# A listed order of steps, replaced by another list, in a one-core kernel of linear attention and a cos-gated MLP

## The chip, the core and the metric

The kernel runs on one core of a Trainium2 chip. The core has TensorE (PE, matmuls and transposes), VectorE (DVE), ScalarE (ACT), GpSimd (POOL) and SyncE (SP), each with its own queue of instructions, which it works off in order. DMAs are issued by SP, ACT and POOL. The metric is the device time of one execution in microseconds; smaller is better.

## What is computed

All inputs are float32. First linear attention for 8 batches, 8 heads, 576 rows and 64 columns, then an MLP on the 4608 rows of 512 that come of it:

```python
def _attn_ref(q, k, v):
    q_s = np.exp(q - np.max(q, axis=-1, keepdims=True))
    q_s = q_s / (np.sum(q_s, axis=-1, keepdims=True) + 1e-09)
    k_s = np.exp(k - np.max(k, axis=2, keepdims=True))
    k_s = k_s / (np.sum(k_s, axis=2, keepdims=True) + 1e-09)
    kv = np.einsum('bhsd,bhse->bhde', k_s, v)
    return np.einsum('bhsd,bhde->bhse', q_s, kv)

def _moe_ref(x, w_in, w_out):
    h = x @ w_in
    g = h * np.cos(h)
    return g @ w_out
```

Between the two, heads and columns are joined to rows of 512. w_in is 512 x 2048, w_out 2048 x 512.

## The kernel before

x is worked off in nine blocks of 512 rows: blocks 0 to 7 are the first 512 rows of each batch, block 8 the 64 rows left of all eight. The attention of a batch runs in two halves of four heads (a = 0, 1; the tiles are `q_0`, `q_1`, `k_0`, `k_1`), and the MLP of a block runs over chunks of 128 of the 2048 hidden columns: h (L1058 at the start, L1066 later), the gate on ACT and DVE (L1091, L1095, L1101, L1106), and its product with w_out into four banks `acc` (L1144, L1151). But for the start, float32 products are made of parts in fp32r: a high and a low part of each operand (`ghi` L1122, `glo` L1126), three matmuls for one. Blocks 5 to 8 are done as two pairs, by seven products of half-size sums in place of eight (L1438 `z` and `a`, with weights and sums of them that are put into DRAM as `w_own` and `w_sums` and loaded back as `s`).

The steps of a half of a batch's attention: `q_max` (L804), then for batch 0's first half 18 exponentials on ACT, each with its own bias and sum (`q_exps`, L817), for all others `q_sub` (L808), one exponential (L812) and a sum (L823); `q_inv` (L827, L828) and `q_norm` (L832). For k: its maximum over rows by three steps on DVE (L694, L699, L703), POOL's all-reduce over partitions (L709, two to a half), `k_sub` (L716) and the exponential (L722). `kv` (L760) multiplies v and k; v has columns of ones beside it, from which `kv_inv` (L768 to L770) makes the divisor, and ACT scales kv by it into `kvw` (L774). q is transposed by PE in batches 0 and 1 (L861, copied by ACT in L865), later by DVE in squares of 32 (`q_blocks`, L880 and L885), through DRAM (`q_rows`, `q_left`). x is the product of `qf` and `kvw` (L913).

Loads of k, q and v have fixed places in SBUF. 576 rows are 4 chunks of 128 and one of 64, the "left" one; in a tile of k the unused 64 rows of that chunk are filled with the lowest float (`frame` in `load_k`, L612, by DVE for batch 0 and by POOL for the others), and v's ones and zeros are set by `v_frame` (L425 to L428). Each load is a main DMA and a left one (k: L617, L620; q: L635, L639, twice; v: L654, L658). The weights come as `raw_i` (L524) and `raw_o` (L529) and are split by L553, L558, L564 and L575. Before PE has real work it runs matmuls on zeros (L739, L1616).

What sets the order: every step is recorded by `plan.add` or `plan.load` with its engine, a duration, what it reads and writes. `Plan.order` could sort them by a list scheduler, with `Plan.lat` as the latency between two steps. A table `ORDER` of all step numbers stands in the file, and it is used instead:

```python
    steps = ORDER or plan.order(CFG["kappa"], CFG["rounds"], CFG["tables"], CFG["alpha"])
```

The steps are then issued in this order, each to its engine's queue, so the table sets the order on every engine. DMA instructions stand in the queue of the engine that issues them, and an SP that waits for a buffer holds every DMA behind it.

Of the kernel before, what the change touches and what calls it, by code (L numbers as in the profile page):

```python
# [215 lines left out]
class Plan:  # L216
# [48 lines left out]
    def lat(self, i, j):  # L265

        a, b = self.steps[i], self.steps[j]
        return self.LAT.get((a[0], b[0]), (a[7] or 1.1) if a[0] == "BUS" else 0.2)
# [89 lines left out]
def linear_attention_then_cos_gated_mlp(  # L358
# [85 lines left out]
    plan = Plan()  # L444
# [161 lines left out]
    def load_k(b, a, place, due, eng="SP"):  # L606
        places = place if isinstance(place, list) else [(place, i) for i in (0, 1)]
# [1093 lines left out]
```

## Time and profile before

| | us |
|---|---|
| median of 3 runs | 863.61 (862.93 to 864.96) |
| profiled execution, its own time | 862.21 |
| its span in the profile | 860.4 |
| PE busy | 844.9 (98%) |
| DVE busy | 600.3 (70%) |
| ACT busy | 491.9 (57%) |
| POOL busy | 71.4 (8%) |

The span runs from the first to the last record; about 1.8 us of the execution lie around it. Engines wait for each other by semaphores; a row of the waits says which engine sat idle before an instruction, and what ended the idle time. A timeline row gives start and length, and in brackets the idle time before it.

### The profile page before, as it was taken

What the parts mean: (1) busy time and instruction counts of PE and PEld (TensorE: products, weight loads), DVE (VectorE), ACT (ScalarE), POOL (GpSimd) and SP (SyncE); (2) the same over time, 40 slices, a digit from 0 to 9 for tenths busy, and PEclk for the clock granted to TensorE, in tenths of its full rate; (3) what the DMA queues carried; (4) which work ended last, traced back from release to release, by engine and by line L of the source; (5) the groups of instructions that cost most, each with busy time, mean ns of one, the idle gap of its engine ahead of it and who ended that gap; (6) DMA issues with size and microseconds to landing.
All of it is one profiled execution on the core that took longest, in us unless ns stands there. A gap on an engine that the chain in (4) does not pass through costs nothing.

```text
span 860.4 us, 12174 instructions
## 1 busy us (share of the span) xinstructions
PE 844.9 (98%) x4340; PEld 664.6 (77%) x4340; DVE 600.3 (70%) x941; ACT 491.9 (57%) x819; POOL 71.4 (8%) x117
## 2 busy tenths in 40 slices
PE   6999999999999999999999999999999999999997
PEld 5644788877877887877877887887888888888886
DVE  5899889986867775776888886784457655444452
ACT  4788788755545546545654657574446544454441
POOL 1200110000001000001000012111100111101000
PEclk8999999999999999999999999999999999999999
DMA  9882474535554454463578837756333546333204
GB/s 237 260 240 102 145 219 127 157 87 162 136 140 112 109 137 135 117 186 114 136 245 258 271 112 216 201 160 189 98 120 123 159 151 180 86 110 109 63 22 126
DMA packets 152381, 130.32 MB, mean 151 GB/s; under 512 B 65536, under 2 KB 125696, under 8 KB 152320
## 3 DMA queue, kind: packets, MB, share of 16 engines
q1 hardware_dynamic: 135456, 98.47, 40.4%
q0 software_dynamic: 13312, 29.36, 11.6%
q10 hardware_dynamic: 3552, 1.70, 0.8%
q8 instruction: 34, 0.56, 0.3%
q14 instruction: 27, 0.22, 0.1%
HBM read 89.92 MB, written 39.58 MB: 151 GB/s over the span
## 4 chain that ended last, share of the span: by engine, by line
PE 92%; DMA 3%; SPq 1%; ACT 1%; DVE 1%; issue 0%; ACTq 0%; DVEq 0%
PE acc L1151 42%; PE h L1066 21%; PE z L1438 10%; PE a L1438 7%; PE h L1058 3%; PE acc L1144 2%; PE kv L760 2%; PE x L913 2%; DMA q<-in_q_dram 2%; ACT q L817 1%; DVE qm L804 0%; PE acc L739 0%; PE qt L861 0%; PE xl L913 0%; SPq L635 0%
## 5 line engine op out<-in xcount | busy, mean ns | idle before, releaser
L1066 PE MATMUL h<-x,w_i 128*128 128x512 f32 x864 | 207.7, 391 | 1.4 <-DVE kt L1106 1.4
L1066 PEld LDWEIGHTS h<-x,w_i 128*128 128x128 f32 x864 | 161.4, 188 | 36.7 <-DVE kt L1106 2.2
L1151 PE MATMUL acc<-w_o,ghi 128*128 128x512 f32 x592 | 184.7, 393 | 0.0
L1151 PEld LDWEIGHTS acc<-w_o,ghi 128*128 128x128 f32 x592 | 109.7, 188 | 29.8 <-issue 5.7
L1151 PE MATMUL acc<-w_o,glo 128*128 128x512 f32 x296 | 115.4, 390 | 0.0
L1438 PE MATMUL z<-xs,s 128*128 128x512 f32 x384 | 97.6, 390 | 0.2 <-DVE glo L1126 0.2
L1091 ACT ACTIVATE kt<-h 128x512 int32<-128x512 f32 x80 | 47.6, 595 | 81.7 <-PE h L1066 67.6
L1438 PEld LDWEIGHTS z<-xs,s 128*128 128x128 f32 x384 | 71.9, 188 | 15.6 <-DVE glo L1126 0.6
L1438 PE MATMUL a<-xs,s 128*128 128x512 f32 x288 | 73.2, 390 | 0.0
L1095 DVE SCALAR_TENSOR_TENSOR kt<-kt,h 128x512 f32<-128x512 int32 x80 | 54.4, 680 | 27.0 <-ACT kt L1091 26.8
L1101 ACT ACTIVATE kt<-kt 128x512 f32<-128x512 f32 x80 | 50.4, 632 | 32.8 <-DVE kt L1095 31.9
L1151 PEld LDWEIGHTS acc<-w_o,glo 128*128 128x128 f32 x296 | 55.6, 188 | 12.0
L1122 ACT CAST ghi<-kt 128x512 fp32r<-128x512 f32 x74 | 45.1, 616 | 31.9 <-PE acc L1151 25.8
L1438 PEld LDWEIGHTS a<-xs,s 128*128 128x128 f32 x288 | 54.0, 188 | 11.2
L1106 DVE TENSOR_TENSOR kt<-kt,h 128x512 f32<-128x512 f32 x74 | 49.9, 678 | 12.5 <-ACT kt L1101 12.0
L1126 DVE TENSOR_TENSOR glo<-kt,ghi 128x512 fp32r<-128x512 f32 x74 | 50.4, 684 | 8.9 <-ACT ghi L1122 8.9
L709 POOL PARTITION_ALL_REDUCE m<-m x32 | 26.0, 856 | 206.5 <-DVE m L703 193.8
L1452 ACT COPY c<-z 128x512 f32<-128x512 f32 x32 | 18.7, 586 | 39.5 <-PE z L1438 28.9
L1459 DVE TENSOR_TENSOR c<-a,c 128x512 f32<-128x512 f32 x32 | 22.0, 688 | 25.2 <-PE a L1438 22.9
L804 DVE TENSOR_REDUCE qm<-q 128x18 f32<-128x1152 f32 x16 | 21.6, 1351 | 20.0 <-DMA q<-in_q_dram 19.8
L1412 POOL DMA_DIRECT2D s<-w_sums x32 | 20.1, 628 | 143.2 <-PE a L1438 120.8
L1412 POOL DMA_DIRECT2D s<-w_own x32 | 20.2, 633 | 117.3 <-PE a L1438 80.1
(631 smaller groups left out, 1415.1 us busy)
## 6 DMA issues: line engine op xcount, KB each, us to landing
s<-w_sums POOLq DMA_DIRECT2D x32, 512.0 KB, 4.7
raw_i<-in_moe_w_in_dram SPq DMA_DIRECT2D x16, 512.0 KB, 7.5
raw_o<-in_moe_w_out_dram SPq DMA_DIRECT2D x16, 512.0 KB, 5.5
s<-w_own POOLq DMA_DIRECT2D x16, 512.0 KB, 4.6
k<-in_k_dram SPq DMA_DIRECT2D x15, 512.0 KB, 4.7
q<-in_q_dram SPq DMA_DIRECT2D x30, 256.0 KB, 3.6
v_sb<-in_v_dram SPq DMA_DIRECT2D x30, 256.0 KB, 4.1
q_rows<-qb SPq DMA_DIRECT2D x96, 64.0 KB, 1.8
```

Source lines behind the costliest of these rows:

```text
L709: nc.gpsimd.partition_all_reduce(T["m", b, a][:, hs].rearrange("p h d -> p (h d)"), T["m1", b, a][:, hs].rearrange("p h d -> p (h d)"), P, ...
L1058: nc.tensor.matmul(o, T["wc", "i", f][:, 0, cs], T["whole"][:, c], start=(c == 0), stop=(c == KC - 1),)
L1066: nc.tensor.matmul(o, a, x, start=(c == 0 and n == 0), stop=(c == KC - 1 and n == 2))
L1091: nc.scalar.activation(t.bitcast(I32), src(), AF.Identity, bias=0.25, scale=1.0 / TWO_PI)
L1095: nc.vector.scalar_tensor_tensor(t, t.bitcast(I32), -TWO_PI, src(), op0=ALU.mult, op1=ALU.add)
L1101: nc.scalar.activation(t, t, AF.Sin, bias=0.5 * math.pi)
L1106: nc.vector.tensor_mul(o, t, src())
L1122: nc.scalar.copy(t, T["g", u])
L1126: nc.vector.tensor_sub(t, T["g", u], T["gh", u].bitcast(F32))
L1151: nc.tensor.matmul(T["acc", j], a[:, js], w, start=(first and n == 0), stop=(last and n == 2))
L1412: nc.gpsimd.dma_start(t, src)
L1438: nc.tensor.matmul(o, a, x, start=(first and c == 0 and m == 0), stop=(c == 1 and m == 2), skip_group_check=not first,)
```

## The change

The table `ORDER` is replaced as a whole: the same steps in another order. Two more lines stand in `Plan.lat`, and the fill of k's unused rows gets a latency for batch 0.

```diff
 ORDER = [
-    2, 9, 12, 46, 7, 8, 4, 5, 13, 10, 6, 51, 17, 18, 14, 11, 15, 16, 27, 28, 29, 39, 52, 53, 21, 54, 19, 30, 131,
...
     def lat(self, i, j):
 
         a, b = self.steps[i], self.steps[j]
+        if a[0] != "BUS" and a[7] is not None and b[0] in ("SP", "BUS", "ACT"):
+            return a[7]
         return self.LAT.get((a[0], b[0]), (a[7] or 1.1) if a[0] == "BUS" else 0.2)
...
-        plan.add("POOL" if b else "DVE", 0.31, frame, writes=places, due=due)
+        plan.add("POOL" if b else "DVE", 0.31, frame, writes=places, due=due, lat=None if b else -99.0)
         plan.load(CFG["bus"]["k"] * 2, load, writes=places, due=due, parts=2, eng=eng)
         return places
```

Line numbers of after are two higher than those of before from `lat` on. The numbers in a tile's name count tiles and differ between the two lists.

SP at the start of the program. `k_0` and `v_0` are batch 0's first half, `q_1` its second; `v_sb` are the two buffers of all later v. ACT's queue issues the four DMAs of `q_0` and two of `k_1` first in both. Before:

```order
L617 DMA k_0_186<-in_k_dram 128x4x256
L620 DMA k_0_186<-in_k_dram 64x4x64
L654 DMA v_0_170<-in_v_dram 128x8x128
L658 DMA v_0_170<-in_v_dram 64x4x64
L635 DMA q_1_197<-in_q_dram 128x8x64
L639 DMA q_1_197<-in_q_dram 64x2x64
L635 DMA q_1_197<-in_q_dram 128x8x64
L639 DMA q_1_197<-in_q_dram 64x2x64
L524 DMA raw_i_202<-in_moe_w_in_dram 128x4x256
L654 DMA v_sb_86<-in_v_dram 128x4x128
```

After:

```order
L619 DMA k_0_182<-in_k_dram 128x4x256
L622 DMA k_0_182<-in_k_dram 64x4x64
L526 DMA raw_i_199<-in_moe_w_in_dram 128x4x256
L637 DMA q_1_201<-in_q_dram 128x8x64
L641 DMA q_1_201<-in_q_dram 64x2x64
L637 DMA q_1_201<-in_q_dram 128x8x64
L641 DMA q_1_201<-in_q_dram 64x2x64
L531 DMA raw_o_214<-in_moe_w_out_dram 128x1024
L656 DMA v_0_216<-in_v_dram 128x8x128
L660 DMA v_0_216<-in_v_dram 64x4x64
L656 DMA v_sb_81<-in_v_dram 128x4x128
```

The first load of w_in now stands ahead of q_1, the first of w_out ahead of v_0, and v_0 behind all of q_1.

DVE at the start, from the first `q_norm` and `k_sub` to the second `k_sub`. Before:

```order
L832 TENSOR_TENSOR q_0_181<-q_0_181,qs_0_195 128x512
L699 TENSOR_TENSOR m_0_1_231<-mt_1_209 128x256
L716 TENSOR_TENSOR k_0_186<-k_0_186,m_0_226 128x1280
L703 TENSOR_TENSOR m_0_1_231<-m_0_1_231,k_1_175 128x256
L827 TENSOR_SCALAR qs_0_195<-qs_0_195 128x10
L828 RECIPROCAL qs_0_195<-qs_0_195 128x10
L804 TENSOR_REDUCE qm_1_248<-q_1_197 128x18
L832 TENSOR_TENSOR q_0_181<-q_0_181,qs_0_195 128x640
L808 TENSOR_TENSOR q_1_197<-q_1_197,qm_1_248 128x1152
L768 TENSOR_REDUCE r_0_305<-kv_0_250 128x2
L769 TENSOR_SCALAR r_0_305<-r_0_305 128x2
L770 RECIPROCAL r_0_305<-r_0_305 128x2
```

The next row is the second `k_sub`. After:

```order
L718 TENSOR_TENSOR k_0_182<-k_0_182,m_0_226 128x1280
L701 TENSOR_TENSOR m_0_1_236<-mt_1_231 128x256
L834 TENSOR_TENSOR q_0_177<-q_0_177,qs_0_187 128x512
L705 TENSOR_TENSOR m_0_1_236<-m_0_1_236,k_1_175 128x256
L829 TENSOR_SCALAR qs_0_187<-qs_0_187 128x10
L830 RECIPROCAL qs_0_187<-qs_0_187 128x10
L806 TENSOR_REDUCE qm_1_278<-q_1_201 128x18
L834 TENSOR_TENSOR q_0_177<-q_0_177,qs_0_187 128x640
L810 TENSOR_TENSOR q_1_201<-q_1_201,qm_1_278 128x1152
L718 TENSOR_TENSOR k_1_175<-k_1_175,m_1_292 128x1280
L770 TENSOR_REDUCE r_0_332<-kv_0_189 128x2
L771 TENSOR_SCALAR r_0_332<-r_0_332 128x2
```

`k_sub` of the first half now stands ahead of the first `q_norm`, that of the second half ahead of `kv_inv`. Besides, v_0's four memsets (L425 to L428), which stood ahead of everything, now stand behind the first `q_max`. On POOL both all-reduces of k_1's maximum now stand ahead of the fill of batch 1's first k. On PE, the four transposes of q's first pair, which followed kv_0, now stand ahead of it; behind kv_1, where a filling of `acc` came first, q_1's transposes follow at once. On ACT, the copy of the first pair's transposes now stands ahead of q_1's exponential, and that of the second pair behind it.

DVE in the middle, in the attention of batch 5 (counted from 0), where q's second half is loaded. `qb` are the buffers of `q_blocks`, `kt` and `glo` belong to the gate. Before:

```order
L880 STREAM_TRANSPOSE qb_0_3338<-q_0_3275 128x512
L885 STREAM_TRANSPOSE qb_0_3338<-q_0_3275 128x128
L1106 TENSOR_TENSOR kt_3259<-kt_3259,h_3246 128x512
L804 TENSOR_REDUCE qm_1_3366<-q_1_3306 128x18
L1126 TENSOR_TENSOR glo_3389<-kt_3213,ghi_3383 128x512
L1095 SCALAR_TENSOR_TENSOR kt_3387<-kt_3387,h_3352 128x512
L880 STREAM_TRANSPOSE qb_1_3393<-q_0_3275 128x512
L1106 TENSOR_TENSOR kt_3387<-kt_3387,h_3352 128x512
```

After:

```order
L1097 SCALAR_TENSOR_TENSOR kt_3256<-kt_3256,h_3212 128x512
L1128 TENSOR_TENSOR glo_3317<-kt_3227,ghi_3309 128x512
L1108 TENSOR_TENSOR kt_3256<-kt_3256,h_3212 128x512
L806 TENSOR_REDUCE qm_1_3353<-q_1_3337 128x18
L1097 SCALAR_TENSOR_TENSOR kt_3320<-kt_3320,h_3296 128x512
L810 TENSOR_TENSOR q_1_3337<-q_1_3337,qm_1_3353 128x1152
L1128 TENSOR_TENSOR glo_3372<-kt_3256,ghi_3322 128x512
L1108 TENSOR_TENSOR kt_3320<-kt_3320,h_3296 128x512
L1097 SCALAR_TENSOR_TENSOR kt_3355<-kt_3355,h_3324 128x512
L882 STREAM_TRANSPOSE qb_1_3389<-q_0_3108 128x512
```

The two rows of `qb_0` stand seven rows ahead of the first of these, so `qb_0` and `qb_1` have 13 rows between them, where there were four.

## Rows read from the trace of the kernel before

**Rows 1.** Page, section 1: busy us, share of span, instructions.

```profile
PE 844.9 (98%) x4340; PEld 664.6 (77%) x4340; DVE 600.3 (70%) x941; ACT 491.9 (57%) x819; POOL 71.4 (8%) x117
```

**Rows 2.** Waits of PE: line waited for, us, times, longest.

```profile
PE kv L760 <- ACT k L722: 5.9, 1, 5.9
PE kv L739 <- DVE v L425: 2.2, 1, 2.2
PE h L1066 <- DVE kt L1106: 1.4, 2, 1.1
PE qt L739 <- ACT qf L865: 0.7, 1, 0.7
PE z L1438 <- DVE glo L1126: 0.2, 1, 0.2
```

**Rows 3.** Windows; last three columns granted clock, DMA share, GB/s.

```profile
0.00:20.00 20.00, 11.83 (x58) 10.57 (x60) 9.88 (x30) 8.66 (x39) 3.45 (x10) 0.92 1.04 228
20.00:25.00 5.00, 4.33 (x51) 3.97 (x52) 4.33 (x7) 2.57 (x5) 1.01 (x2) 0.64 0.87 266
25.00:60.00 35.00, 35.00 (x260) 20.09 (x259) 30.96 (x54) 29.98 (x53) 3.49 (x5) 1.00 0.84 249
```

**Rows 4.** Chain of waits, 0 to 50: start us, us, what.

```profile
2.97 8.14 DMA q<-in_q_dram
...
11.23 1.36 DVE qm L804
...
16.85 1.84 ACT q L817 x11
18.69 1.17 ACT k L722
...
19.90 2.44 PE kv L760 x40
...
23.43 1.17 ACT qf L865 x2
...
26.69 1.02 PE x L913 x8
27.71 1.32 PE kv L760 x40
```

**Rows 5.** Timeline, 355 to 369, all engines: start, us, engine, line, operation.

```profile
366.92 0.71 DVE L880 STREAM_TRANSPOSE qb<-q 128x512 f32<-128x512 f32 x1 [2.30 <-DMA q_left<-qb]
...
368.26 0.96 PE L1066 MATMUL h<-x,w_i 128*128 128x512 f32 x3 [1.14 <-DVE kt L1106]
```

**Rows 6.** Timeline of SP, 0 to 26: issues.

```profile
0.73 0.46 SPq L617 DMA_DIRECT2D k<-in_k_dram  x1
...
2.21 0.64 SPq L654 DMA_DIRECT2D v<-in_v_dram  x1
```

**Rows 7.** Timeline of DVE, 0 to 36.

```profile
2.29 0.28 DVE L426 MEMSET v<- 64x264 f32 x1
...
2.77 0.55 DVE L612 MEMSET k<- 64x256 f32 x2
...
16.90 1.48 DVE L716 TENSOR_TENSOR k<-k,m 128x1280 f32<-128x1280 f32 x1
...
22.93 0.17 DVE L770 RECIPROCAL r<-r 128x2 f32<-128x2 f32 x1
23.69 1.49 DVE L716 TENSOR_TENSOR k<-k,m 128x1280 f32<-128x1280 f32 x1 [0.60 <-POOL m L709]
25.68 1.35 DVE L823 TENSOR_REDUCE qs<-q 128x18 f32<-128x1152 f32 x1 [0.50 <-ACT q L812]
...
28.08 1.36 DVE L832 TENSOR_TENSOR q<-q,qs 128x1152 f32<-128x1152 f32 x1
```

**Rows 8.** DMA view, 0 to 20: KB each, median us to landing.

```profile
v<-in_v_dram SPq DMA_DIRECT2D x1, 512.0 KB, 7.6
```

**Rows 9.** Waits of DVE.

```profile
DVE qm L804 <- DMA q<-in_q_dram: 19.8, 9, 7.9
```

289 rows, old and new, of the table ORDER are left out of this document.

## The prediction

> **What bounds the kernel now.** I read four views, from the whole to the place. The page's first section says that TensorE (PE) is busy 844.9 us of a span of 860.4 us [rows 1]: the program is a queue of matmuls, and an order can only win back what PE stands idle or runs slowly. No step is added or removed, every engine keeps its instructions and their sizes, so those 844.9 us stay but for the clock. PE's waits [rows 2] add to about 10.4 us: 5.9 for the exponential of k (`k_exp`, L722), 2.2 for the first memsets, 1.4 and 0.2 in the middle of the program, 0.7 for the copies of q's transposes (L865). Three of these five rows, 8.8 us, are the start: nothing else is large enough to be worth a table. In the windows [rows 3] PE is busy 11.83 of the first 20 us, 4.33 of the next 5 at a granted clock of 0.64 of full speed, and 35.00 of the 35 after that: whatever the order does for the start is decided by about 28 us.
>
> The chain through the start [rows 4] shows who waits for whom. The last piece of q of batch 0's first half (q_0, issued on ACT's queue) takes 8.14 us and is there at 11.11. DVE takes its maximum (1.36), ACT runs 18 separate exponentials on it, the last of them ending at 18.69, and only then the exponential of k (1.17). At 19.90 PE can form kv_0 (v times k, L760), which takes 2.44 us, where the same kind of product, kv_1, is done in 1.32 at 27.71: after the pause PE is granted half its clock. Then follow q's transposes, the copies of them (23.43), 16 filling matmuls, x at 26.69, and kv_1 at 27.71. In the middle, two rows [rows 5] show the other kind of wait: at 366.92 DVE has stood 2.30 us in `q_blocks` (L880) because the puts of an earlier q buffer had not landed, and PE lost 1.14 behind it at 368.26, since the next gate product (kt, L1106) is queued behind that row on DVE.
>
> **The change, part by part. The planner's lines** in `Plan.lat` and the -99 in `load_k` are costs that `Plan.order` reads. The kernel takes `ORDER` (L1661), so the built program shows nothing of them: 0. The load of k_0 was already issued at 0.73 us [rows 6], and DVE filled the unused rows at 2.77 [rows 7]. Taking the fill from before that load can win nothing at the start.
>
> **SP's loads at the start.** v_0 leaves its place behind k_0, where it was issued at 2.21 [rows 6], and goes behind raw_i, all of q_1 and raw_o; its memsets leave the idle time before 11 us and now follow q_0's maximum on DVE. On q_0's landing, which moves the whole chain one for one: what ran beside q_0 was v_0 (512 and 64 KB) and then q_1's first piece. Now it is raw_i (512 KB) and q_1, whose second half (288 KB) can come some us earlier. At the 228 GB/s of the first 20 us [rows 3], 64 KB less ahead of it is 0.3 us; 288 KB more, half of whose time falls on q_0 if the two queues share the engines, is 0.6. So -0.3 to +0.6; I take 0, because the bytes of the first SP load are almost the same and what follows is uncertain in both directions.
>
> The profile gives the order in which pieces landed, not the share of each queue: q_0's last piece took 8.14 us with v_0 beside it [rows 4]. The Trainium skill, DMA: Bandwidth & Descriptors, section "Queues, rings and completion order", says that each DMA engine goes round between the queue rows for which it has work, packet by packet. That speaks against issuing q_1 on SP's queue while q_0 is still coming on ACT's: by it the sum would take the upper end, +0.6, and without it 0.
>
> **DVE in the start.** q_0's maximum ends at 12.6. The four memsets of v_0 (0.28 for the largest [rows 7], about 0.5 in all) now stand there, so the three steps of k's maximum and POOL's all-reduce of it come 0.5 later, and `k_sub` of k_0 starts at about 16.5. It began at 16.90 before, since it stood behind the first `q_norm` (0.61 to the next row) and one step of k_1's maximum (0.33); these now follow it. The exponential of k still waits for ACT's 18 exponentials until 18.69, so kv_0 cannot start before 19.9. The gain must come behind that. DVE has no idle time from 16.9 to the end of `kv_inv` (22.93 + 0.17 = 23.10 [rows 7]). After the change `k_sub` of k_1 (1.49, some 1.4 to the next row) stands ahead of `kv_inv`. Before, it came behind and waited 0.60 for POOL, whose all-reduce of k_1's maximum was queued behind a memset of the next k; both all-reduces now stand ahead of that memset. So `kv_inv` ends at 23.10 - 0.4 + 0.6 + 0.3 + 1.4 = 25.0. ACT scales kv by it (0.5 in all), and x can start at 25.6 instead of 26.69: **-1.1**. The exponential of k_1 (1.2) follows on ACT and lets kv_1 start at 26.75 instead of 27.71: **-0.95**. The copies that held x before are done by then, because the transposes of q's first pair now stand ahead of kv_0 and their copy ahead of q_1's exponential (all of it ended by 24.8). The fills of two banks lie in the wait for 25.6.
>
> What is late next? v_0. It can be issued from 12.7 on. The one row of such a load says 7.6 us to landing, with q_0 and k_1 beside it [rows 8], so 20.3 for the main part and 21.0 for the rest: later than 19.9. But kv_0's result is wanted by `kv_inv` only at 24.3, and kv_0 takes 2.4, so it may start as late as 21.9 at no cost. Behind kv_1 PE now goes on with q_1's transposes, with no fill between. They need q_1's sum and norm on DVE (1.35 and 1.36 [rows 7], and 0.5 for the inverse): 25.0 + 3.2 = 28.2, where kv_1 ends at 28.1. That is 0.1 of wait. **The start: -1.0**, with q_0's landing -1.3 to -0.4.
>
> **The middle.** The three waits, 1.6 us together, had causes that the new order moves: the two `q_blocks` rows between which q_1's maximum stood now have 13 rows between them instead of four. On the other side every other place is new too. The page shows what is exposed: nine waits of DVE for q cost it 19.8 us, 7.9 of it at the start [rows 9], and nearly all were hidden because PE had other rows ready. Where the new neighbours hide less, a wait reaches PE. With bounds of -1.6 (all gone, none new) and +3 (two of DVE's 2.3 us waits with half their length or more uncovered, the old ones gone) I take 0: the same loads, puts and buffers, the same number of places. **The tail**, from the last matmul to the last put, keeps its steps: 0.
>
> **Sum.** -1.0 on the profiled execution of 862.21 us gives 861.2. That execution lies 1.4 below the median of the runs, 863.61; the median should move by the same 1.0, to **862.6**.
>
> **The rivals.**
> (1) The start gains and the middle's waits go as well: -1.0 - 1.6 = -2.6, 861.0. For it: the 1.14 us of [rows 5] hung on two rows of DVE that now stand apart. Against: every stretch of the middle has other places as thin.
> (2) The start's gain is given back by transfers. The DMA engines have a share of 0.87 and 0.84 from 20 to 60 us [rows 3], and the weights and the next k still have to come; if PE reaches their consumers a microsecond earlier it waits a microsecond there, 863.6. The same time comes out if the change does not do what it says: the lines on k's fill act on nothing, and k's load was first already. Against: PE had no idle time at all from 25 to 60, so there is slack in front of these loads, if of unknown size.
> (3) Slower: DVE stands before a load or a put (`q_max` or `q_blocks`) at two places with nothing ready for PE. It decides when the gate chain queued behind that row has less matmul work ahead of it than the 2.3 us of the wait [rows 5]. Price 2 x 2.3 = 4.6 with the old waits kept: -1.0 + 4.6 = +3.6, 867.2. One such place gives +1.3, 864.9, which is within 0.2%; so it takes two. For it: in the trace of before 2.30 us of DVE already cost PE 1.14. Against: beyond the start, the waits for q cost PE at most a part of that 1.14.
>
> **How the numbers follow.** A measurement of this kernel can tell about 0.2%, 1.7 us, from no change: faster means below 861.9, slower above 865.3. My forecast (862.3 to 863.2) has 0.48, the first rival 0.23, the second 0.16, the third 0.13. Faster: the first rival and some of the forecast's lower end with a middle that gains in part, 0.32. Slower: the third and a little for mixtures of it, 0.15. Same: the rest, 0.53. The range reaches from the first rival, with the best of q_0's landing and some scatter, 860.4, to just above one uncovered place, 865.4; left out are most of the third rival and the far end of the first.
>
> **What would show it.** Right: in the chain of after, q_0 lands between 10.8 and 11.7 us, kv_0 still starts at 19.9 to 21, x at 25.6 and kv_1 at 26.8; the row of PE waiting for L865 is gone and one for the scaled kv (L774), or for DVE through it, stands there. v_0 lands at 18 to 21. In the middle, PE's waits sum to 0 to 3 us. Wrong: kv_0 after 22 (v_0 late), q_0 after 12 (shared queues), new PE waits above 3 us behind 60, or busy time of PE other than 844.9 by more than 1.

## The result: slower, against the forecast

The changed kernel takes 869.29 us (median, 868.38 to 869.9), the kernel before, timed beside it, 863.27 (862.71 to 864.96): a ratio of 1.0066, with a 95% interval of 1.0048 to 1.0083. The forecast was 862.6, with a range of 860.4 to 865.4. The profiled execution took 869.47 us, with a span of 867.7, which is 7.3 longer than that of before.

The first section of the page says something that the forecast had ruled out:

```profile
PE 849.0 (98%) x4340; PEld 664.5 (77%) x4340; DVE 599.9 (69%) x941; ACT 492.7 (57%) x819; POOL 73.1 (8%) x117
```

The same 4340 matmuls are busy 4.1 us longer than in [rows 1]. So "busy" holds waiting. Where it does, a later row will show. PE's open waits, as in [rows 2]:

```profile
PE qt L863 <- DMA v_sb<-in_v_dram: 5.4, 1, 5.4
PE qt L741 <- DVE zero L1613: 2.2, 1, 2.2
PE kv L762 <- DMA v_sb<-in_v_dram: 1.6, 1, 1.6
PE acc L1153 <- ACT o L1198: 1.3, 2, 0.9
PE z L1440 <- ACT c L1454: 0.7, 1, 0.7
PE z L1440 <- ACT ghi_('s', 1, 3, 0)_6941 L1124: 0.5, 1, 0.5
PE z L1440 <- DMA s<-w_own: 0.5, 1, 0.5
PE h L1068 <- DVE kt L1108: 0.5, 1, 0.5
PE a L1440 <- DVE kt_('s', 0, 2, 3)_5189 L1108: 0.4, 1, 0.4
```

The first two are the start. The 5.4 is named after a DMA that ended last by the records; the transposes behind that wait read the first `q_norm`, which ended on DVE at 19.25. The other seven lines add to 5.5 us, where before had 1.6 beyond the start, and only one of them is of a kind that before had. The wait of 1.1 us at 368 us that the first rival wanted gone is gone.

**The start came at the times worked out, by another path.** DVE, ACT's scaling of kv, and PE in the changed kernel (timelines; start, us, engine, line):

```profile
11.51 1.35 DVE L806 TENSOR_REDUCE qm<-q 128x18 f32<-128x1152 f32 x1 [8.71 <-DMA q<-in_q_dram]
...
16.82 1.49 DVE L718 TENSOR_TENSOR k<-k,m 128x1280 f32<-128x1280 f32 x1 [0.71 <-POOL m L711]
...
23.14 1.48 DVE L718 TENSOR_TENSOR k<-k,m 128x1280 f32<-128x1280 f32 x1
...
24.94 0.17 DVE L772 RECIPROCAL r<-r 128x2 f32<-128x2 f32 x1
```

```profile
25.14 0.52 ACT L776 ACTIVATE kvw<-kv,r 128x64 f32<-128x64 f32 x2 [0.24 <-DVE r L772]
```

```profile
20.52 2.44 PE L762 MATMUL kv<-v,k 128*64 128x66 f32 x40
...
23.78 2.33 PE L741 MATMUL qt<-zero 128*128 128x128 f32 x16
26.04 1.09 PE L915 MATMUL x<-qf,kvw 64*64 64x512 f32 x8
...
27.06 1.39 PE L762 MATMUL kv<-v_sb,k 128*64 128x66 f32 x40
```

The same rows of PE's timeline in the kernel before:

```profile
24.64 2.05 PE L739 MATMUL qt<-zero 128*128 128x128 f32 x16 [0.68 <-ACT qf L865]
26.62 1.09 PE L913 MATMUL x<-qf,kvw 64*64 64x512 f32 x8
27.64 1.39 PE L760 MATMUL kv<-v_sb,k 128*64 128x66 f32 x40
```

q_0's maximum begins 0.28 later than in [rows 4], inside the bounds of -0.3 to +0.6; `kv_inv` ends at 25.1 (25.0 was worked out, without the 0.28), and kv_1 begins at 27.06 (26.75 plus 0.28), 0.58 earlier than before. v_0 landed 5.3 us after its issue and held nothing. But x did not wait for the scaled kv. That was done at 25.66 (25.14 + 0.52), and x began at 26.04, when the 16 filling matmuls in front of it had run. PE's wait for the copies of q's transposes (L865 before, L867 now) is gone, as forecast; the wait for L774 that the forecast wanted in its place is not in the list above.

**The middle lost.** Counted from the start of one matmul to the next, less the usual 0.23, the changed kernel loses about 9.5 us at twelve places behind 40 us, before about 2.0 at three. With the 0.6 that the start gains this is 6.9 of the 7.3 us. Three places show the kinds.

At 239 us stands the x product of batch 3's first half, eight matmuls in one row of PE's timeline. The first fence is the changed kernel, the second the one before:

```profile
238.97 2.13 PE L915 MATMUL x<-qf,kvw 64*64 64x512 f32 x8
```

```profile
245.26 1.09 PE L913 MATMUL x<-qf,kvw 64*64 64x512 f32 x8
```

Nothing in brackets, so no wait is told, but the row is 1.04 longer. SP issued the load of its second operand (qf_1) only at 236.37, since the puts that it reads back had just landed, and it took 3.5 us: 239.9. The first two matmuls had their operand and ran, the other six stood behind the load, and the row counts as busy throughout. A second such row is at 472.47 (2.12 us). These two are half of the 4.1 us of additional busy time; another 1.0 is the start, where PE is busy 4.52 us instead of 4.03 from 10 to 20 us, and 9.88 instead of 9.32 from 20 to 30. PE's waits do not list the two rows; the length of a row against the same row of before shows them.

At 414 kv waits for v. SP's timeline ahead of it, and PE's row:

```profile
404.51 1.63 SPq L656 DMA_DIRECT2D v_sb<-in_v_dram  x1
406.18 0.65 SPq L660 DMA_DIRECT2D v_sb<-in_v_dram  x1
406.87 0.59 SPq L971 DMA_DIRECT2D x_main<-xs  x1
407.51 1.84 SPq L1211 DMA_DIRECT2D out_dram<-o  x4
409.39 0.68 SPq L1289 DMA_DIRECT2D w_own<-w_i  x1
410.12 0.63 SPq L656 DMA_DIRECT2D v_sb<-in_v_dram  x1
```

```profile
414.36 1.39 PE L762 MATMUL kv<-v_sb,k 128*64 128x66 f32 x40 [1.64 <-DMA v_sb<-in_v_dram]
```

Six puts stand between the two loads of v in SP's queue; the second is issued at 410.12, 2.6 us before its product could have begun (414.36 - 1.64 = 412.72).

At 554 the first pair's products wait for the banks of block 4. ACT's and PE's timelines:

```profile
553.90 0.59 ACT L1198 COPY o<-acc 128x512 f32<-128x512 f32 x1 [2.13 <-DMA out_dram<-o]
```

```profile
554.54 0.73 PE L1153 MATMUL acc<-w_o,ghi_('s', 0, 0, 2)_4992 128*128 128x512 f32 x2 [0.88 <-ACT o L1198]
```

The copy of a finished bank waits for the puts of an earlier one, because there are two buffers; with the copy, every gate step behind it on ACT.

### The profile page after: what moved, and what is told of

It reads as the page before. It is cut to its first block, busy times and chain, and to the rows that moved or that the text cites. A ratio compares the mean times of both kernels' runs of the same rounds, so it can differ in the third digit from the quotient of the medians.

```text
span 867.7 us, 12159 instructions
## 1 busy us (share of the span) xinstructions
PE 849.0 (98%) x4340; PEld 664.5 (77%) x4340; DVE 599.9 (69%) x941; ACT 492.7 (57%) x819; POOL 73.1 (8%) x117
## 5 line engine op out<-in xcount | busy, mean ns | idle before, releaser
L1108 DVE TENSOR_TENSOR kt<-kt,h 128x512 f32<-128x512 f32 x74 | 50.4, 681 | 18.1 <-ACT kt L1103 17.6
```

The costliest lines, as they stand in the source:

```text
L1108: nc.vector.tensor_mul(o, t, src())
```

## Experiments

In the diffs, `before` and `after` are the two lists of steps, and `[:75]` means the first 75 steps that issue something. A step's number names it in both.

**The start alone.**

```diff
-ORDER = before
+ORDER = after[:75] + [i for i in before if i not in after[:75]]
```

> The first 75 steps come in the changed order (through the second kv product and the first transposes after it), all others in the order of before. Theory A (the changed kernel loses its time at single places of the middle and the pairs, each on its own, and its start is a gain): kv_1 at about 27.1 us instead of 27.7, PE's later waits those of before, time 0.6 us below before, 862.7. Rival B (the earlier start moves all that follows against transfers that do not move, and so opens the later waits): new waits of PE above 2 us in sum behind 60 us, time 1 to 5 us above before.

861.95 us against 863.07, a ratio of 0.9982 (0.9971 to 0.9992). The start is a gain, of 1.1 us in the medians, and the only new wait behind it is one of 0.3 us. Theory A holds in the time; rival B falls. The run's own profile does not show where the 1.1 comes from. PE's timeline in it:

```profile
23.95 2.62 PE L739 MATMUL qt<-zero 128*128 128x128 f32 x16
...
27.52 1.39 PE L760 MATMUL kv<-v_sb,k 128*64 128x66 f32 x40
```

kv_1 begins 0.1 earlier than before, not the 0.6 that was expected: the granted clock from 20 to 25 us was 0.50 in this execution, 0.64 in that of before, and the filling matmuls took 2.62 us instead of 2.05.

**The middle alone.**

```diff
-ORDER = before
+ORDER = before[:75] + after[:1521] + before, each step once
```

> Order of before, but for the steps between the second kv product and the first product of the first pair (about 27 to 520 us), which come in the changed order. Theory A: the waits of the changed kernel in that stretch come back although the start is that of before (x pairs broken at about 239 and 472, kv waiting for v at about 412, h at 457), about +5.0, and the 1.7 us of before go: +3.3, 866.6. Rival B: with the old start they close, within 1 us of before.

867.16 us, a ratio of 1.0043 (1.0029 to 1.0057): +4.1. The waits are there with the old start too; here the x product of 239 us is split, and the second part's wait is told in part (0.33 of 1.4 us):

```profile
241.97 1.07 PE L913 MATMUL x<-qf,kvw 64*64 64x512 f32 x2
243.38 1.08 PE L913 MATMUL x<-qf,kvw 64*64 64x512 f32 x6 [0.33 <-DMA qf<-q_rows]
```

In this profile, 5.2 us longer than that of before, the start takes 2.0: the filling matmuls at 24.75 ran 3.79 us, where before has 2.05, and the granted clock from 25 to 30 us was 0.62, in before 1.00 (more on this below). The 3.2 left are what was expected (3.3). Whether the same accounts for the 0.8 that the medians lie above it is not shown.

**The pairs alone, and all but the pairs.**

```diff
-ORDER = before
+ORDER = before[:1521] + [i for i in after if i not in before[:1521]]
```

> Order of before up to the first product of the first pair (about 520 us), the changed order from there. Theory A: waits of PE at the change from block 4 to the pair, in the first pair for c, s and part, and one in the second pair, 4.6 us in sum against 0.3 of before: +4.3, 867.6. Rival B: with the old start they close, within 1 us of before.

870.9 us, a ratio of 1.0087 (1.0056 to 1.0119): +7.8, more than the whole change; there are four runs, from 868.5 to 873.0. One wait belongs to the joint of the two lists alone:

```profile
523.60 0.70 PE L1438 MATMUL z<-xs,s 128*128 128x512 f32 x2 [2.82 <-DMA s<-w_sums]
```

Without it about 5 are left. The opposite half has no such joint:

```diff
-ORDER = after
+ORDER = after[:1521] + [i for i in before if i not in after[:1521]]
```

> The changed order up to the first product of the first pair (about 520 us), the order of before from there: the other half of e3_new_pairs, which lost 3.0 us at its own joint (s load at 520). Theory A: the waits of the pairs of the changed kernel (4.6 us) go and those of before (0.3) come: 869.3 - 4.3 = 865.0. Theory E (the pairs' order costs what e3_new_pairs showed, 7.8): 861.5.

866.05 us against 863.57, a ratio of 1.0031 (1.0013 to 1.0049): +2.5, where the start alone and the middle alone add to -1.1 + 4.1 = 3.0. The two parts do add, within the interval (1.1 to 4.2 us). What is left of the whole change is the pairs: 869.29 - 866.05 = 3.2 us.

**Mends in the changed order.** Four waits are taken away by moving five steps.

```diff
-999 (x of batch 3, first half), 791, 790
+791, 790, 999
...
-1691 (x of batch 6, second half), 1430 (acc)
+1430, 1691
...
-1635 (load of v), 1603, 1047, 1276 (puts), 1633 (load of v)
+1635, 1633, 1603, 1047, 1276
...
-1900, 1902, 1872, 1879, 1905 (ACT's copy and gate steps), 1507, 1510 (copies of finished banks)
+1510, 1507, 1900, 1902, 1872, 1879, 1905
```

> The changed order with three mends: x of batch 3's first half goes behind the next two acc products on PE, x of batch 6's second half behind the next acc unit; on SP the load of the last v of batch 6 goes ahead of the put of x, four output puts and a stash put; on ACT the two copies of block 4's first finished banks go ahead of two gate steps and a copy. Theory A: the four waits mended (1.04 + 1.04 + 1.8 + 1.0) come off one for one, 869.3 - 4.9 = 864.4, and the other waits stay where they are. Rival C (the middle is bound by something with a rate, such as transfers or ACT, so that a wait taken away comes back at the next place): 867 to 869, with new waits right behind the mended ones.

865.85 us, a ratio of 1.0023 (1.001 to 1.0035) to before and 3.4 less than the changed kernel. All four waits are gone. Of the 4.9 us hoped for, 1.5 came back: neither theory alone. In the profile about as much stands at three rows of h that wait for the gate product: 0.47 at 417 and 0.31 at 469, both new, and 1.29 at 458 where the changed kernel has 0.49. PE's and DVE's timelines of the mended kernel, where kv no longer waits:

```profile
412.05 1.39 PE L762 MATMUL kv<-v_sb,k 128*64 128x66 f32 x40
...
416.86 0.50 PE L1068 MATMUL h<-x,w_i 128*128 128x512 f32 x1 [0.47 <-DVE kt L1108]
...
457.79 3.02 PE L1068 MATMUL h<-x,w_i 128*128 128x512 f32 x12 [1.29 <-DVE kt L1108]
```

```profile
408.05 1.35 DVE L806 TENSOR_REDUCE qm<-q 128x18 f32<-128x1152 f32 x1 [2.45 <-DMA q<-in_q_dram]
...
416.15 0.65 DVE L1108 TENSOR_TENSOR kt<-kt,h 128x512 f32<-128x512 f32 x1
```

In the changed kernel the gate product comes at the same time:

```profile
416.24 0.65 DVE L1108 TENSOR_TENSOR kt<-kt,h 128x512 f32<-128x512 f32 x1
```

DVE stood 2.45 us for q before 408 (1.95 in the changed kernel). In the changed kernel PE stood for v meanwhile and came later to the product that needs the gate; with v early PE meets the late gate product instead.

**What in the start gained.** The start's engines without its loads, and its loads alone:

```diff
-SP = after's loads, v_0's memsets (9) behind q_max, raw_o's first steps (144, 145) early on ACT
+SP = before's loads, 9, 144, 145 where before has them
```

> The changed order of the start on PE, DVE, ACT and POOL, but SP's loads as before (so v_0's memsets stay ahead of q_0's maximum, and raw_o's first two steps on ACT stay where they were). Theory A (the start's gain is DVE's and POOL's order, the loads cost a little through q_0): q_0 lands at 11.1, x at 25.3 to 25.6, kv_1 at 26.5 to 26.8, 1.0 us below before, 862.1. Rival D (the gain comes from the loads of w_in and w_out ahead of v_0 and q_1): nothing left, kv_1 within 0.2 of 27.7, 863.1.

861.17 us, a ratio of 0.9972 (0.9961 to 0.9983): -1.8. PE's timeline:

```profile
18.56 1.09 PE L861 MATMUL qt<-ident,q 128*128 128x128 f32 x4 [4.18 <-ACT q L817]
19.77 2.44 PE L760 MATMUL kv<-v,k 128*64 128x66 f32 x40
...
23.05 2.57 PE L739 MATMUL qt<-zero 128*128 128x128 f32 x16
25.55 1.09 PE L913 MATMUL x<-qf,kvw 64*64 64x512 f32 x8
26.57 1.39 PE L760 MATMUL kv<-v_sb,k 128*64 128x66 f32 x40
```

ACT's scaling of kv:

```profile
24.24 0.52 ACT L774 ACTIVATE kvw<-kv,r 128x64 f32<-128x64 f32 x2 [0.24 <-DVE r L770]
```

x and kv_1 come 1.1 earlier than in [rows 4], as the forecast's sum said, without q_0's 0.28. Here too x is held by the filling matmuls: the scaled kv was ready at 24.76. The 0.7 of the 1.8 beyond this is not seen in the trace, whose span is 0.9 shorter than that of before. It may be the clock: among the runs with a mean granted clock of 0.995 or more the medians are 861.3 and 862.4, 1.1 apart.

```diff
-SP = before's loads of the start
+SP = after's loads of the start, all other engines as before
```

> SP's loads of the start in the changed order (raw_i ahead of q_1, raw_o ahead of v_0, v_0 behind all of q_1), every other engine in the order of before. Theory A: q_0 lands 0.3 later (11.4), the chain with it, kv_1 at 28.0, 863.4. Rival D: kv_1 earlier than 27.5, 862.3 or less.

862.94 against 863.01, 0.9999 (0.9987 to 1.0011): nothing. So the new place of v_0 and of the weights gains nothing, and beside the reordered engines the time is 0.8 higher with it (861.95 against 861.17). The profiles of the start alone and of the start without its loads take this apart: with the new loads q_0's maximum begins 0.57 later (11.66 and 11.09), and `k_sub` 1.10 later (16.97 and 15.87), so that 0.53 come in behind q_0's maximum, where the four memsets now stand. Rival D falls.

**A kernel below both.** The last wait of before at 368 us was mended on top of the new start.

```diff
-1086, 1087, 1576 (square transposes), 1088 (gate product)
+1086, 1087, 1088, 1576
```

> The changed order of the start, all else in the order of before, and one step of DVE moved: the gate product of chunk 53 goes ahead of the square transposes of batch 5's second q, which waited for puts. Theory A (a wait of PE behind a DVE row that waits for a DMA goes when the row is moved behind the gate): the wait at 366 goes, 1.1 us less than the new start alone, 860.9, below both kernels. Rival C (it comes back at the next row): 861.9, a new wait within 10 us behind.

863.46 us, 0.9998 (0.9985 to 1.001): the wait at 368 is gone, and the median is 1.5 us above that of the start alone, though the two intervals overlap. Rival C was right on the wait, 10.7 us behind the old one, and too low in its time (861.9):

```profile
378.98 1.69 PE L913 MATMUL x<-qf,kvw 64*64 64x512 f32 x8 [0.92 <-DMA qf<-q_rows]
```

The row is 0.60 longer than the 1.09 of before besides, so that 1.5 us stand here for the 1.1 mended. PE comes sooner to the x product of that batch, and the chain of square transposes, puts and loads that feeds it comes no sooner, but somewhat later. The last attempt moves that x product as well, on the start without its loads:

```diff
-1088 behind 1576, 1581 (x of batch 5, first half) ahead of 1107 (acc)
+1088 ahead of 1576, 1581 behind 1107
```

> The start of s1_start_no_loads (new order of the engines, loads as before), the gate product of chunk 53 ahead of the square transposes as in f1_new_start_one_mend, and the x product of batch 5's first half behind the next acc unit (2.7 us), so that it does not meet the later qf load. Theory A': the mend of f1 moved the puts, and the wait went to x; with x moved as well both waits are gone: 1.1 us less than s1, 860.1. Rival C (the loss goes on to the next place again): 861 to 862, with a wait of PE of over 0.5 us between 365 and 400.

861.07 us, 0.9979 (0.9965 to 0.9992), within the interval of the start without its loads (861.17): the loss went on to the second half's x.

```profile
395.05 1.07 PE L913 MATMUL x<-qf,kvw 64*64 64x512 f32 x2
396.67 1.08 PE L913 MATMUL x<-qf,kvw 64*64 64x512 f32 x6 [0.55 <-DMA qf<-q_rows]
```

The start of this kernel is that of the run without its loads, and a second profile of it tells what x waits for. The scaled kv is ready at 24.76 in both; x begins 0.41 earlier, as the filling matmuls run 0.41 shorter:

```profile
23.05 2.16 PE L739 MATMUL qt<-zero 128*128 128x128 f32 x16
25.14 1.09 PE L913 MATMUL x<-qf,kvw 64*64 64x512 f32 x8
```

So the version to keep is the start without its loads: the new order there on PE, DVE, ACT and POOL, all loads and all that follows as before, 861.17 us, 1.8 below before and 8 below the changed kernel.

## Why the prediction was wrong

**The start was right in its number, and by another path than the one named.** -1.0 was forecast, -1.1 measured alone, and v_0 landed in time. The forecast let x wait for the scaled kv, through POOL, `k_sub` and `kv_inv`, with the filling matmuls inside that wait. `kv_inv` did end at 25.1, but the filling matmuls lay behind it: x began 0.4 to 0.8 us after the scaled kv was ready (25.66 and 26.04 in the changed kernel, 25.82 and 26.50 with the start alone, 24.76 and 25.55, 24.76 and 25.14 without its loads), and each time as the fill ended. What gained is PE's own order: the wait of 0.68 for the copies of q's transposes is gone, and four of the eight transposes lie ahead of kv_0, where PE had stood. The forecast had the first of these; that x and kv_1 came within 0.2 us of its times, once the 0.28 of q_0 is added, is in part luck. No run has PE's order alone, so this is read from the traces.

**q_0's landing** was taken as 0 in the sum, between -0.3 and +0.6. In the changed kernel's profile it is 0.28. Over all profiles it is the upper end: q_0's maximum begins at 11.51 to 11.82 in the six with the new loads, and at 11.07 to 11.23 in the five with the old ones, 0.6 between the middles. The Trainium skill (DMA: Bandwidth & Descriptors, "Queues, rings and completion order") says that each DMA engine goes round, packet by packet, between the queue rows that have work for it. The traces agree with it in sign and with the size that the forecast gave for it.

**The step that failed** is "The middle", where the term was taken as 0, because "the same loads, puts and buffers, the same number of places" were at work. It measured +7.3 (4.1 and 3.2), more than twice the upper bound of +3. Two things were wrong with that step. First, the order of before had hidden nearly every DMA, and this other list of the same steps did not leave the sum of waits even; whether most lists would lose is not shown by one. Second, the bound was made of one kind of wait, DVE before a load of q, since before showed that kind. The waits that came were of others: qf to x, v to kv, puts to ACT's copies, s to z, ACT's steps to z. Only 0.9 us (the two rows of L1108) stood behind the gate product on DVE.

**The premise "those 844.9 us stay but for the clock"** fell too. Busy time rose by 4.1: half of it is the two rows of x that count as busy while their later matmuls wait for an operand, and 1.0 is the start.

**The rivals.** The first (the middle's old waits go) was right in its wait, the 1.1 at 368, and wrong in its sum, since new ones came. The second (given back by transfers) is not what happened to the start: alone, it keeps its gain. The third gave the right side and nearly the size (867.2), by the wrong mechanism and with a chance of 0.13. Rival B of the experiments, that the earlier start opens the waits, is excluded: the middle and the pairs have them behind the old start too.

**What stays open** is why the new list places these steps so closely; the experiments show where and how much, not what its maker's costs were. The waits at 571 to 598 and at 787 us were not mended singly.

## What to carry to other kernels

When a tuned order is replaced, the term for "all the rest" has no value of 0: follow each load, put and read-back to its consumer, count what stands between them in the queue, and give what can't be followed a loss as its middle value. Take such a change apart by splicing the two lists; one part of a losing change may be a gain. A mended wait gives back its own length only if the next engine was not late behind it: look for what was catching up during the wait before moving a step.

## What the runs showed of the hardware

The granted clock at the start is not the same in every execution of the same program, and part of the spread goes with it. In the profile of the run with the start's loads alone (the order of PE is that of before) the granted clock from 25 to 30 us was 0.52, the lower of the two levels (1.2 of 2.4 GHz) through nearly all of it; ahead of that PE had stood from about 13.7 to 20.4. The 16 filling matmuls took 3.79 us. In the profile of before, shown above, the same 16 took 2.05. Its row in PE's timeline, and its window (last columns granted clock, DMA share, GB/s):

```profile
25.44 3.79 PE L739 MATMUL qt<-zero 128*128 128x128 f32 x16 [0.67 <-ACT qf L865]
```

```profile
25.00:30.00 5.00, 4.56 (x24) 3.79 (x24) 4.16 (x6) 3.02 (x5) 0.00 (x0) 0.52 0.75 215
```

Over 78 executions of the kernel before, the 20 with a mean granted clock of 0.996 or more have a median of 862.3 us, the 15 with 0.992 or less one of 864.6. At first sight the new start makes this spread smaller: 861.4 to 862.7 for the start alone and 860.4 to 862.0 without its loads, against 861.7 to 866.0 of before beside the first. But the last attempt, with that same start and two steps moved, runs from 859.3 to 864.4, so that the start steadies the time is not shown.
